# Attention with rotary embedding and a routed expert layer: probabilities turned by VectorE in 32x32 blocks, value products on eight tiles of TensorE

## The chip, the cores and the metric

One core of a Trainium2 chip. The metric is the device time of one execution in microseconds (us); the kernel before has run three times. Engines: TensorE (PE, with PEld for its weight loads), VectorE (DVE), ScalarE (ACT), GpSimd (POOL), SyncE (SP, which here only issues transfers).

## The reference

Attention over 8 batches, 8 heads, 576 positions and 64 dimensions, all float32, then a layer in which 128 tokens of each batch pass through an expert:

```python
q_rot, k_rot = rotate(q), rotate(k)            # rotary embedding
scores = np.matmul(q_rot, k_rot.transpose(0, 1, 3, 2)) / np.sqrt(D)
attn = np.exp(scores - scores.max(-1, keepdims=True))
attn = attn / (attn.sum(-1, keepdims=True) + 1e-09)
x = np.matmul(attn, v)                          # heads side by side: (B, 576, 512)
s = np.einsum('bsd,d->bs', x, w_gate)
# of each batch the 128 tokens with the highest s: x += sigmoid(s) * relu(x @ w1) @ w2
```

## The kernel before

The unit of work is a pair of heads: 32 pairs, four to a batch. For each pair, `load` (line 451) issues the transfers of k, q and v on SyncE; `rotate` (line 472) forms the rotary embedding on POOL (the first pair's on DVE); `split_qk` (line 502) splits k and q into a high and a low float32r part on ACT and on POOL or DVE. `attend` (line 528) does the attention. Its nine units (`UNITS`) are 128 queries of one head each, units 2t and 2t+1 being the two heads of query tile t, and unit 8 the last 64 queries of both heads. `units` (line 537) makes the scores of two units at a time: the two heads contract 64 dimensions on two row tiles of PE, and three products (high x high, high x low, low x high) of two halves of 288 keys go into two PSUM banks a unit. `softmax` (line 566) takes the negated maximum on DVE (`nm`), and the exponential with its sum on ACT, into `pab` (unit 8 into `pr`) in SBUF.

The value product contracts over keys, so that keys must lie on partitions, and the probabilities have queries there. `turn` (line 583) transposes a unit on PE, four blocks of 128x128 into a bank, and copies the bank to `pt` on ACT or DVE; `turn_rem` (line 607) does the last 64 keys, into `pk`. `value` (line 638) then multiplies, in two halves of the queries (c = 0 with 256 columns, c = 1 with 320): five blocks of 128 keys, for each of which the two heads run side by side on two column tiles of PE, v being the stationary operand:

```python
for kt in range(NT + 1):
    for h in range(2):
        nc.tensor.matmul(bank_of(acc)[hp, 0:n], lt, rt, start=kt == 0, stop=kt == NT)
```

Its result has dimensions on partitions; it is copied out (`ot`), transposed back on PE, and multiplied by the reciprocal sums on DVE into the output rows `x`. After each batch, `route` (line 758) ranks the tokens with many small DVE operations, gathers the 128 rows, and two chained products with `w1` and `w2` update them.

The order of all this is written by a planner (`Order`, line 71). Every operation is given engines, estimated durations, a key, and what it waits for; the planner goes through time and gives each free engine the ready operation with the lowest key, and `issue` (line 228) then emits each engine's instructions in that order, which is fixed. Keys are a time (20,000 a pair) plus offsets from the table `KEY`. `Banks` gives out the eight PSUM banks: a unit takes two neighbours ("wide"), everything else one. All instructions are recorded by one helper, so that the profile gives them one line, 211 (223 in the change).

Of the kernel before, what the change touches and what calls it, by code (L numbers as in the profile page):

```python
# [22 lines left out]
KEY = dict(ahead=6669, lag=12977, rem=76, value=4203, rows=388, load=49858, rotate=24073, half=2000,  # L23
           gate=54405, route=49769, count=21851, select=23426, turn=18811, step=10093, kstep=3, hold=2,
           patience=7975, over=350, near=3316, narrow=195)


SWITCH = ((0.0, 175.0, 194.0), (151.0, 0.0, 196.0), (151.0, 125.0, 0.0))

# [7 lines left out]

class Banks:


    def __init__(self, n):
        self.free, self.n, self.narrow = [0.0] * n, n, 0

    def when(self, kind, count=1):
        if kind == "wide":
            pairs = sorted(max(self.free[i], self.free[i + 1]) for i in range(0, self.n, 2))
            return pairs[count - 1]
        return 1e12 if self.narrow + count > KEY["narrow"] else sorted(self.free)[count - 1]

    def take(self, kind, t):  # L50
        if kind == "wide":
            i = min((max(self.free[i], self.free[i + 1]), i) for i in range(0, self.n, 2))[1]
            self.free[i] = self.free[i + 1] = 1e12
            return i
        self.narrow += 1
        i = min((self.free[i ^ 1] <= t, self.free[i], i) for i in range(self.n) if self.free[i] <= t)[2]
        self.free[i] = 1e12
        return i

    def give(self, kind, slot, at):  # L60
        self.narrow -= kind != "wide"
        for i in range(slot, slot + 1 + (kind == "wide")):
            self.free[i] = at
# [7 lines left out]
class Order:  # L71
# [26 lines left out]
    def run(self):  # L98
# [18 lines left out]
        while events:  # L117
# [4 lines left out]
            while moved:  # L122
                moved = False
                for e in names:
                    if free[e] > t:
                        continue
                    put, found, soon, first = [], None, None, None
                    while waiting[e]:
# [10 lines left out]
                        if e == "DVE" and o.mode == 2:  # L139
                            can = max(can, free["POOL"])  # L140
                        if can > t:
                            if o.urgent and can < t + KEY["patience"] and (soon is None or can < soon):
                                soon = can
                        elif soon is None or t + o.engines[e][0] <= soon + KEY["over"]:
                            if e != "PE" or o.mode == mode or (mode and o.mode):
                                found = o
                                break

                            first = first or o
                        if first and o.key > first.key + (KEY["near"] if mode else 0):  # L150
                            put.append(item)
                            break
                        put.append(item)
                    for item in put:
                        heapq.heappush(waiting[e], item)
                    found = found or first
# [5 lines left out]
                    if o is first:  # L162
                        o.done = True
# [64 lines left out]
def issue(tc, nc, order):  # L228
# [6 lines left out]
    for _, _, o, e in order:  # L235
# [5 lines left out]
        held = [i for b in o.banks for i in range(b.slot, b.slot + 1 + (b.kind == "wide"))]  # L241
        real = [i for s in held for other, i in last.get(s, {}).items() if other != e]
        keep = real + [i for a in needs.get(id(o), ()) for i in made[id(a)]]
        groups = sorted({s // 2 for s in held})
        for i in mine:
            for g in groups:
                for other in {"PE", "ACT", "DVE"} - {e}:
                    tc.declare_no_dep(i, group=f"bank{g}{other}", keep=keep, reason="other half of the tile")
# [4 lines left out]
        for i in mine:  # L253
            for g in groups:
                tc.add_to_no_dep_group(f"bank{g}{e}", i)
# [26 lines left out]
def attention_moe_kernel(ctx: ExitStack, tc: tile.TileContext, q, k, v, w_gate, w1, w2, rope, outs, cap):  # L282
# [18 lines left out]
    B, H, S, D = v.shape  # L301
    DM = H * D
    F = w1.shape[1]
    NP = H // 2
# [3 lines left out]
    KW = S + REM  # L308
    NDC = DM // P
# [14 lines left out]
    ps_banks = [ps.tile([P, 2, 512], F32, name=f"ps{i}") for i in range(4)]  # L324

    order = Order(2 * len(ps_banks))
# [33 lines left out]
    def bank_of(b):  # L360
        two = ps_banks[b.slot // 2]
        return two if b.kind == "wide" else two[:, b.slot % 2]
# [5 lines left out]
    tabk = sb("tabk", [P, 2, KW])  # L368
# [7 lines left out]
    k_ins = ring("k_in", 2, [P, 2, KW])  # L376
    rks = ring("rk", 1, [P, KW])
    rqs = ring("rq", 1, [P, KW])
    khs = ring("kh", 2, [P, KW], F32R)
    kls = ring("kl", 2, [P, KW], F32R)  # L380
    qhs = ring("qh", 2, [P, KW], F32R)
    qls = ring("ql", 2, [P, KW], F32R)
    vts = ring("vt", 3, [P, 2, NT, D])
    vrs = ring("vr", 3, [P, 2, D])
    pabs = ring("pab", 4, [P, 2 * S])
    prs = ring("pr", 1, [P, KW])
    pts = [ring(f"pt{c}", 1, [P, NT, 2, 2 * P + c * REM]) for c in range(2)]
    pks = [ring(f"pk{c}", 1, [P, 2 * P + c * REM]) for c in range(2)]
    ots = [ring(f"ot{c}", 1, [P, 2 * P + c * P]) for c in range(2)]
    xs = ring("x", 2, [P, 5, DM // 2])  # L390
    sumss = ring("sums", 3, [P, 9, 2])
    nms = ring("nm", 2, [P, 9])
    rss = ring("rs", 2, [P, 6])
# [20 lines left out]
    for t_ in vrs.tiles:  # L414
        nc.gpsimd.memset(t_[64:128, 0, :], 0.0)
        nc.gpsimd.memset(t_[0:64, 1, :], 0.0)
    nc.gpsimd.memset(ots[1].tiles[0][:, 2 * P + REM:3 * P], 0.0)
    nc.gpsimd.memset(prs.tiles[0][:, S:KW], 0.0)
# [24 lines left out]
    KCUTS, QCUTS = (0, REM + HALF, KW), (0, P, 3 * P, KW)  # L443
# [5 lines left out]
    loaded, rotated, stacks = {}, {}, {}  # L449

    def load(pi):
        b, j = divmod(pi, NP)
        key = at(pi, 0) - KEY["load"]
        main = lambda src: src[b, 2 * j:2 * j + 2, 0:512, :].rearrange("h (p t) d -> p h t d", t=NT)
        rem = lambda src, h: src[b, 2 * j + h, 512:S, :]
        kin, qin, vt, vr = k_ins.next(), q_ins.next(), vts.next(), vrs.next()
        got = {"k": [], "q": [], "v": []}
# [6 lines left out]
        for n, use, src, cuts in ("k", kin, k, KCUTS), ("q", qin, q, QCUTS):  # L464
            for i, (lo, hi) in enumerate(zip(cuts, cuts[1:]) if pi == 0 else [(0, KW)]):
                dma(n, use.tile[:, :, lo:hi], src[b, j, :, :, lo:hi], use, 2 * i + (n == "q"), 8 * P * (hi - lo))
        dma("v", vt.tile, main(v), vt, 5, 8 * P * NT * D)
        for h in range(2):
            dma("v", vr.tile[h * 64:h * 64 + 64, h, :], rem(v, h), vr, 5, 64 * 4 * D)
        loaded[pi] = (kin, qin, vt, vr, got)  # L470

    def rotate(pi):

        kin, qin, _, _, got = loaded[pi]
        first = pi == 0
        key = at(pi, 0) - KEY["rotate"]
        rk, rq = rks.next(), rqs.next()
        made = {}

        def tt(on, n, out, in0, in1, alu, after, uses, soon):  # L480
# [4 lines left out]
            for u in uses:  # L485
                u.by(o)
            return o

        for name, use, r, tab, cuts in (("k", kin, rk, tabk, KCUTS), ("q", qin, rq, tabq, QCUTS)):
            x = use.tile  # L490
            made[name] = []
            for i, (lo, hi) in enumerate(zip(cuts, cuts[1:]) if first else [(0, KW)]):
# [3 lines left out]
                       [got[name][i]] + tab_ready[name][i] if first else got[name] + sum(tab_ready[name], []), [use], soon)  # L496
                made[name].append((lo, hi, tt(
                    e, hi - lo, r.tile[:, lo:hi], x[:, 0, lo:hi], x[:, 1, lo:hi], ALU.add, [y] + r.before, [use, r], soon)))
        rotated[pi] = (rk, rq, made)


    def split_qk(pi):
        rk, rq, made = rotated.pop(pi)
# [4 lines left out]
        for n, (name, r, hu, lu) in enumerate((("k", rk, kh, kl), ("q", rq, qh, ql))):  # L508
# [564 lines left out]
```

## Time and profile before

| | |
|---|---|
| runs | 651.12 us median (649.14 to 651.22) |
| profiled execution | 648.06 us, its span 646.3 us |
| PE busy | 610.5 us, 94% |
| DVE busy | 492.8 us, 76% |
| POOL busy | 447.2 us, 69% |
| ACT busy | 413.6 us, 64% |

The span reaches from the first to the last instruction; the execution's own time is 1.7 us longer. Busy times count an engine's records, which overlap where it is pipelined. A record's duration is thus more than its share of a dense run; that share is the distance between two starts.

### The profile page before, as it was taken

How to read it: one execution, taken by the hardware profiler on the slowest of the kernel's cores; microseconds unless marked ns; L12 is line 12 of the kernel's file. 1: busy time of each engine (PE TensorE's matmuls, PEld its weight loads, DVE VectorE, ACT ScalarE, POOL GpSimd, SP SyncE). 2: the span in 40 equal slices, each digit the busy share in tenths (PEclk: the TensorE clock that was granted, in tenths of full speed). 3: DMA queues.
4: the chain of work that ended last, by engine and by line, in shares of the span. 5: the costliest groups of instructions: out<-in, count | busy, mean ns of one | idle time of the engine just before them, and what ended most of it. 6: DMA issues, size and time to landing. Idle time of an engine off the chain costs nothing.

```text
span 646.3 us, 13873 instructions
## 1 busy us (share of the span) xinstructions
PE 610.5 (94%) x5072; PEld 470.4 (73%) x5072; DVE 492.8 (76%) x1264; ACT 413.6 (64%) x989; POOL 447.2 (69%) x308
## 2 busy tenths in 40 slices
PE   3889879999999999999999999999999999999895
PEld 3567667777787777777777877877777787777574
DVE  6898878987879578885869758795878868697541
ACT  4578756777777576665776657675767657765211
POOL 4988788999998989687785678776785845300110
PEclk9999989999999999999999999999999999999999
DMA  8546514343344243333431234242332312010200
GB/s 304 183 168 217 165 57 140 125 137 120 134 142 137 75 158 99 100 119 117 144 110 56 100 127 144 83 137 71 125 124 71 119 36 72 19 38 2 70 31 18
DMA packets 38180, 71.02 MB, mean 110 GB/s; under 512 B 7776, under 2 KB 26976, under 8 KB 38112
## 3 DMA queue, kind: packets, MB, share of 16 engines
q1 hardware_dynamic: 36288, 65.29, 30.9%
q0 software_dynamic: 1280, 4.20, 1.9%
q8 instruction: 40, 0.66, 0.4%
q10 hardware_dynamic: 544, 0.66, 0.3%
q14 instruction: 28, 0.23, 0.1%
HBM read 58.59 MB, written 11.53 MB: 108 GB/s over the span
## 4 chain that ended last, share of the span: by engine, by line
PE 72%; DVE 16%; issue 6%; ACT 3%; DMA 1%; POOL 0%; POOLq 0%; DVEq 0%; ACTq 0%; SPq 0%
PE ps L211 72%; DVE nm L211 5%; DVE junk L211 4%; ACT pab L211 2%; DVE pt L211 2%; DVE x L211 1%; DVE w L211 1%; DMA k_in<-k_dram 1%; DMA xe<-w_dram 1%; DVE ql L211 0%; DVE row L211 0%; DVE ht L211 0%; DVE rs L211 0%; DVE pk L211 0%; DVE gp L211 0%
## 5 line engine op out<-in xcount | busy, mean ns | idle before, releaser
L211 DVE TENSOR_REDUCE nm<-ps 128x1 f32<-128x576 f32 x288 | 206.6, 748 | 88.1 <-PE ps L211 87.2
L211 ACT ACTIVATE pab<-ps,nm 128x576 f32<-128x576 f32 x256 | 188.1, 740 | 102.7 <-DVE nm L211 101.6
L211 PE MATMUL ps<-ident,pab 128*128 128x128 f32 x1152 | 163.0, 279 | 7.3 <-ACT pab L211 6.9
L211 PEld LDWEIGHTS ps<-ident,pab 128*128 128x128 f32 x1152 | 132.6, 143 | 20.6 <-ACT pab L211 7.5
L211 PE MATMUL ps<-pt,vt 128*64 128x320 f32 (+1 forms) x1024 | 138.2, 412 | 0.9 <-DVE pk L211 0.9
L211 ACT COPY pt<-ps 128x512 f32<-128x512 f32 x156 | 88.7, 593 | 30.9 <-PE ps L211 29.6
L211 POOL TENSOR_TENSOR k_in<-k_in,tabk 128x1280 f32<-128x1280 f32 x31 | 90.6, 2923 | 21.5 <-DMA k_in<-k_dram 21.4
L211 PEld LDWEIGHTS ps<-pt,vt 128*64 128x64 f32 x1024 | 67.9, 136 | 49.4 <-issue 8.9
L211 PE MATMUL ps<-kh,qh 64*128 64x288 f32 (+1 forms) x576 | 85.2, 344 | 13.5 <-ACT qh L211 8.1
L211 POOL TENSOR_TENSOR q_in<-q_in,tabq 128x1280 f32<-128x1280 f32 x31 | 90.9, 2933 | 5.6 <-DMA q_in<-q_dram 5.6
L211 DVE COPY pt<-ps 128x512 f32<-128x512 f32 x132 | 86.9, 680 | 6.5 <-PE ps L211 6.2
L211 PEld LDWEIGHTS ps<-kh,qh 64*128 64x128 f32 (+1 forms) x576 | 49.0, 188 | 55.5 <-ACT pab L211 22.7
L211 POOL TENSOR_TENSOR kl<-rk,kh 128x640 fp32r<-128x640 f32 x29 | 45.1, 1555 | 55.7 <-ACT kh L211 55.6
L211 PE MATMUL ps<-kh,ql 64*128 64x288 f32 (+1 forms) x576 | 69.7, 295 | 0.2 <-DVE ql L211 0.2
L211 PE MATMUL ps<-kl,qh 64*128 64x288 f32 (+1 forms) x576 | 69.2, 294 | 0.0
L211 POOL TENSOR_TENSOR prod<-x,wg 128x512 f32<-128x512 f32 (+1 forms) x45 | 49.0, 1088 | 25.8 <-DVE gp L211 18.9
L211 PE MATMUL ps<-w,xt 128*128 128x512 f32 x192 | 52.1, 412 | 1.0 <-ACT xt L211 0.7
L211 PEld LDWEIGHTS ps<-kh,ql 64*128 64x128 f32 (+1 forms) x576 | 52.4, 188 | 0.5 <-DVE ql L211 0.5
L211 PEld LDWEIGHTS ps<-kl,qh 64*128 64x128 f32 (+1 forms) x576 | 52.4, 188 | 0.0
L211 PE MATMUL ps<-w,ht 128*128 128x512 f32 x192 | 51.3, 406 | 0.5 <-DVE ht L211 0.5
L211 POOL TENSOR_TENSOR rq<-q_in 128x640 f32<-128x640 f32 x31 | 48.5, 1565 | 3.7 <-DVE ql L211 3.5
L211 ACT ACTIVATION_READ_ACCUMULATOR pab<-ps,nm 128x1 f32 x256 | 50.9, 199 | 0.0
(98 smaller groups left out, 809.9 us busy)
## 6 DMA issues: line engine op xcount, KB each, us to landing
k_in<-k_dram SPq DMA_DIRECT2D x31, 640.0 KB, 3.8
q_in<-q_dram SPq DMA_DIRECT2D x31, 640.0 KB, 4.3
vt<-v_dram SPq DMA_DIRECT2D x32, 256.0 KB, 2.7
out_dram<-x SPq DMA_DIRECT2D x16, 512.0 KB, 3.4
xe<-w_dram SPq DMA_DIRECT2D x8, 256.0 KB, 3.5
row<-w_dram SPq DMA_DIRECT2D x8, 256.0 KB, 3.1
vr<-v_dram SPq DMA_DIRECT2D x64, 16.0 KB, 2.4
out_dram<-x SPq DMA_DIRECT2D x16, 64.0 KB, 3.1
```

Of the source, the lines that this page charges most:

```text
L211: i = made(*args, **kwargs)
```

## The change

Probabilities no longer pass through PE to be turned. The nine units of a pair lie in one tile `prob` of 128 partitions by nine slots of 576, two such tiles in turn. Behind each exponential DVE transposes the slot in place, in blocks of 32x32: within each group of 32 partitions a block then has keys on partitions and queries along it. `turn` and `turn_rem`, `pab`, `pr`, `pt` and `pk` are gone.

`value` runs once a pair. The block of 32 keys number kb lies in all four partition groups a, there for the 32 queries a of each query tile. Each group is a row tile of PE (32 rows), and each head a column tile (64 columns), so that there are eight products for each of 18 key blocks, of five or four slots of 32 columns (160 or 128), and each row tile adds up in a PSUM bank of its own: four neighbouring banks, 0 to 3, a new kind "quad". v is needed on all four partition groups, so the host lays it out four times (`_by_key`), and it is loaded in two halves (`load_v`).

```diff
+            y = op({"DVE": dve(S)}, lambda: nc.vector.transpose(dst, dst), key + KEY["lag"], [x])
+            prob.by(x, y)
+            turned.append(y)
+
+        def value(key, late):
+            acc, b, br = Bank("quad"), Bank("t"), Bank("t")
...
+            def products(i):
+                for c in range(NB // 2):
+                    for a in range(4):
+                        for h in range(2):
+                            hp, ap = slice(64 * h, 64 * h + 64), slice(32 * a, 32 * a + 32)
+                            s0, s1 = (0, NT + (a < 2)) if h == 0 else (NT + (a < 2), U)
+                            to = 32 if s0 != NT else 0
+                            kb = i * NB // 2 + c
+                            nc.tensor.matmul(
+                                bank_of(acc)[hp, a, to:to + 32 * (s1 - s0)].rearrange("p (s c) -> p s c", c=32),
+                                vt[i].tile[ap, c, h, :], prob.tile[ap, s0:s1, kb * 32:kb * 32 + 32],
+                                start=kb == 0, stop=kb == NB - 1)
+
+            o = None
+            for i in range(2):
+                o = op(pe(NB // 2 * 280), lambda i=i: products(i), key, turned + [got[i], o], acc, mode=1)
...
-                dma("v", vt.tile, main(v), vt, 5, 8 * P * NT * D)
...
+            o = op(LOAD, lambda use=use, src=src: nc.sync.dma_start(use.tile, src),
+                   at(pi, 0) - KEY["load"] + 5 + i, use.before, moved=8 * P * NB // 2 * D)
...
+def _by_key(v):
+    B, H, S, D = v.shape
+    t = v[:, :, _columns(S)].reshape(B, H // 2, 2, S // 32, 32, D).transpose(0, 1, 4, 3, 2, 5)
+    return np.tile(t, (1, 1, 4, 1, 1, 1))
```

Smaller edits: k loses 64 doubled columns (640 to 576), the rotated k and q overwrite their input tiles instead of `rk` and `rq`, output rows are scaled in one operation for four query tiles and one for the rest, `KEY` has other values, and the planner may leave PE in its tiling mode at a cost taken from that table (`STAY`). While a quad waits for its banks, other work gets banks 4 to 7 only.

What the planner makes of it, on DVE in the second pair of heads. `nm` are maxima, `pt` and `pk` copies of transposed probabilities, `rs` reciprocal sums. Before:

```order
L211 TENSOR_REDUCE nm_115<-ps_64 128x1
L211 COPY pt_103<-ps_66 128x4x128
L211 COPY pk_105<-ps_63 128x256
L211 COPY pt_104<-ps_63 128x8x64
L211 TENSOR_REDUCE nm_115<-ps_65 128x1
```

and now, `prob` being the probabilities:

```order
L223 TENSOR_REDUCE nm_99<-banks 128x1 x4
L223 STREAM_TRANSPOSE prob_91<-prob_91 128x576
L223 TENSOR_REDUCE nm_99<-banks 128x1 x2
L223 STREAM_TRANSPOSE prob_91<-prob_91 128x576 x2
L223 TENSOR_REDUCE rs_101<-sums_96 128x9
```

The copies between the maxima have given way to block transposes; over the whole program 288 of them come, and 132 copies into `pt` on DVE and 156 on ACT go.

On PE, at the end of a pair, `ident` being the identity against which a block is transposed. Before, the first pair:

```order
L211 MATMUL ps_65<-ident,pr_102 128x128 x4
L211 MATMUL ps_65<-ident,pab_101 128x128 x8
L211 MATMUL ps_64<-ident,pab_100 128x128
L211 MATMUL ps_64<-ident,pab_101 128x128
L211 MATMUL ps_64<-ident,pr_102 128x128 x2
L211 MATMUL ps_64<-pt_104,vt_92 64x320 x8
L211 MATMUL ps_64<-pk_106,vr_95 64x320 x2
L211 MATMUL ps_66<-kh_85,qh_89 128x288
```

and now, a later pair, the scores of the next one and then the first key block:

```order
L223 MATMUL banks<-kh_80,qh_84 128x288 x4
L223 MATMUL banks<-kl_82,qh_84 128x288 x4
L223 MATMUL banks<-kh_80,ql_86 128x288 x4
L223 MATMUL banks<-prob_90,vt_88 64x160
L223 MATMUL banks<-prob_90,vt_88 64x128
L223 MATMUL banks<-prob_90,vt_88 64x160
L223 MATMUL banks<-prob_90,vt_88 64x128 x2
L223 MATMUL banks<-prob_90,vt_88 64x160
L223 MATMUL banks<-prob_90,vt_88 64x128
L223 MATMUL banks<-prob_90,vt_88 64x160 x2
```

The transposes that stood ahead of the value products are gone, and the products, ten of 256 and ten of 320 columns a pair, are now 144 of 128 or 160.

The end of the last batch on DVE. `junk` are comparisons that rank tokens of the batch before the last, `x` output rows, `ht` a hidden layer's low part. Now, behind the last maximum:

```order
L223 TENSOR_REDUCE nm_99<-banks 128x1 x2
L223 TENSOR_TENSOR x_94<-banks,rs_100 128x4x128
L223 TENSOR_TENSOR x_94<-banks,rs_100 64x128
L223 STREAM_TRANSPOSE prob_91<-prob_91 128x576
L223 SCALAR_TENSOR_TENSOR junk_121,gp_104<-x_94,wg 128x128
...
L223 TENSOR_REDUCE rs_101<-sums_96 64x1
L223 RECIPROCAL rs_101<-rs_101 128x10
L223 STREAM_TRANSPOSE prob_91<-prob_91 128x576
L223 TENSOR_SCALAR junk_122,cnt_111<-row_110,sc_109 128x320
L223 TENSOR_SCALAR junk_122,cnt_111<-row_110,sc_109 128x384
```

Before, those comparisons stood some forty rows ahead of the last maximum; now five of them, the rank and the selection come behind it, as do the last two transposes.

## Rows read from the trace of the kernel before

**Rows 1.** The page's head, busy times and the SyncE queue
```profile
span 646.3 us, 13873 instructions
...
PE 610.5 (94%) x5072; PEld 470.4 (73%) x5072; DVE 492.8 (76%) x1264; ACT 413.6 (64%) x989; POOL 447.2 (69%) x308
...
q1 hardware_dynamic: 36288, 65.29, 30.9%
```

**Rows 2.** The page's chain that ended last, by engine
```profile
PE 72%; DVE 16%; issue 6%; ACT 3%; DMA 1%; POOL 0%; POOLq 0%; DVEq 0%; ACTq 0%; SPq 0%
```

**Rows 3.** Groups by shape: operands, shapes, count | busy us, mean ns | idle before, releasers
```profile
L211 DVE TENSOR_REDUCE nm<-ps 128x1 f32<-128x576 f32 x288 | 206.6, 748 | 88.1 <-PE ps L211 87.2 <-ACT pr L211 0.6
...
L211 PE MATMUL ps<-ident,pab 128*128 128x128 f32 x1152 | 163.0, 279 | 7.3 <-ACT pab L211 6.9 <-DVE x L211 0.2
...
L211 DVE COPY pt<-ps 128x512 f32<-128x512 f32 x132 | 86.9, 680 | 6.5 <-PE ps L211 6.2
...
L211 DVE TENSOR_TENSOR x<-ps,rs 128x256 f32<-128x256 f32 x64 | 26.5, 415 | 4.6 <-PE ps L211 4.6
...
L211 DVE TENSOR_REDUCE gp<-prod 128x2 f32<-128x512 f32 x30 | 20.1, 669 | 0.0
...
L211 DVE TENSOR_TENSOR ht<-ps,ht 128x512 fp32r<-128x512 f32 x16 | 10.9, 683 | 8.1 <-ACT ht L211 8.0
...
L211 DVE TENSOR_TENSOR ql<-rq,qh 128x640 fp32r<-128x640 f32 x6 | 7.2, 1206 | 0.0
```

**Rows 4.** PE's timeline, merged: start us, us, engine, operation, count [idle before]
```profile
87.42 0.66 PE L211 MATMUL ps<-ident,pab 128*128 128x128 f32 x4 [3.49 <-ACT pab L211]
...
305.36 0.27 PE L211 MATMUL ps<-tok,sel 128*128 128x5 bf16 x5
305.49 0.42 PE L211 MATMUL ps<-ident,pab 128*128 128x128 f32 x2
...
307.66 2.38 PE L211 MATMUL ps<-pt,vt 128*64 128x320 f32 x16
...
310.50 0.53 PE L211 MATMUL ps<-kh,qh 64*128 64x288 f32 x4
...
312.32 2.01 PE L211 MATMUL ps<-ident,pab 128*128 128x128 f32 x16
314.17 0.60 PE L211 MATMUL ps<-ident,pr 128*128 128x128 f32 x4
...
316.12 1.95 PE L211 MATMUL ps<-pt,vt 128*64 128x256 f32 x16
...
318.43 0.53 PE L211 MATMUL ps<-kh,qh 64*128 64x288 f32 x4
```

**Rows 5.** PE's timeline of 307.66 to 307.67 us
```profile
307.66 0.49 PE L211 MATMUL ps<-pt,vt 128*64 128x320 f32 x2
```

**Rows 6.** DVE's timeline, early and late
```profile
46.33 2.73 DVE L211 TENSOR_REDUCE nm<-ps 128x1 f32<-128x576 f32 x4
...
58.32 2.47 DVE L211 COPY pt<-ps 128x512 f32<-128x512 f32 x4
...
595.25 0.74 DVE L211 TENSOR_REDUCE nm<-ps 128x1 f32<-128x576 f32 x1
...
608.78 0.17 DVE L211 TENSOR_REDUCE sc<-gp 128x5 f32<-128x15 f32 x1
```

**Rows 7.** Windows: busy us (instructions) of PE, PEld, DVE, ACT, POOL, clock, DMA
```profile
0.00:11.80 11.80, 2.59 (x18) 2.24 (x20) 7.03 (x31) 4.35 (x9) 2.67 (x20) 1.00 0.83 288
11.80:596.00 584.20, 568.06 (x4852) 438.52 (x4850) 465.65 (x1151) 399.43 (x960) 438.12 (x278) 1.00 0.34 112
596.00:646.30 50.30, 39.80 (x210) 29.64 (x208) 20.14 (x85) 9.82 (x20) 6.39 (x11) 0.96 0.12 39
40.00:60.00 20.00, 18.11 (x168) 14.29 (x169) 18.79 (x35) 15.93 (x40) 18.77 (x12) 1.00 0.47 151
80.00:100.00 20.00, 16.40 (x135) 12.48 (x133) 15.97 (x25) 11.11 (x30) 18.07 (x10) 0.91 0.27 92
```

More of the change, by code (lines that the diff above doesn't have):

```diff
@@ L144, in run @@
                         elif soon is None or t + o.engines[e][0] <= soon + KEY["over"]:
[L145 to L151, printed above, removed]
+                            late = o.key + (STAY[mode][o.mode] if e == "PE" else 0)
+                            if first is None or late < least:
+                                first, least = o, late
+                        put.append(item)
+                        if first and o.key >= least:
                             break
-                        put.append(item)
+                    found = first
                     for item in put:
-                        heapq.heappush(waiting[e], item)
-                    found = found or first
+                        if item[2] is not found:
+                            heapq.heappush(waiting[e], item)
                     if found is None:
@@ L240, in issue @@
             continue
-        held = [i for b in o.banks for i in range(b.slot, b.slot + 1 + (b.kind == "wide"))]
+        held = [i for b in o.banks for i in range(b.slot, b.slot + WIDTH[b.kind])]
         real = [i for s in held for other, i in last.get(s, {}).items() if other != e]
         keep = real + [i for a in needs.get(id(o), ()) for i in made[id(a)]]
-        groups = sorted({s // 2 for s in held})
         for i in mine:
-            for g in groups:
-                for other in {"PE", "ACT", "DVE"} - {e}:
-                    tc.declare_no_dep(i, group=f"bank{g}{other}", keep=keep, reason="other half of the tile")
+            for other in {"PE", "ACT", "DVE"} - {e}:
+                tc.declare_no_dep(i, group=f"banks{other}", keep=keep, reason="other banks of the tile")
         for r in {r.name for r in real}:
@@ L253, in issue @@
         for i in mine:
[L254 to L255 removed]
+            tc.add_to_no_dep_group(f"banks{e}", i)
         for s in held:
@@ L322, in ring @@
         return Ring([sb(f"{name}{i}", shape, dtype) for i in range(n)])
-    ps_banks = [ps.tile([P, 2, 512], F32, name=f"ps{i}") for i in range(4)]
-    order = Order(2 * len(ps_banks))
+    banks = ps.tile([P, 8, 512], F32, name="banks")
+    order = Order(8)
     op = order.op
@@ L638, in value @@
-        def value(c, key, late):
-            n = 2 * P + c * REM
-            acc, b = Bank("t"), Bank("t")
-            ot, rs = ots[c].next(), rss.next()
-            def products():
-                for kt in range(NT + 1):
-                    for h in range(2):
-                        hp = slice(64 * h, 64 * h + 64)
-                        lt, rt = ((vt.tile[:, h, kt, :], pt[c].tile[:, kt, h, :]) if kt < NT
-                                  else (vr.tile[:, h, :], pk[c].tile))
-                        nc.tensor.matmul(bank_of(acc)[hp, 0:n], lt, rt, start=kt == 0, stop=kt == NT)
-            o = op(pe((NT + 1) * 2 * (n * 2 / 2.4 + 2.5)), products, key, evacs[c] + got["v"], acc, mode=1)
-            for use in (vt, vr, pt[c], pk[c]):
-                use.by(o)
-            e = op(either(n), lambda e: copy(e, ot.tile[:, 0:n], bank_of(acc)[:, 0:n]), key, [o] + ot.before, acc)
-            w = 4 + c
+            y = op({"DVE": dve(S)}, lambda: nc.vector.transpose(dst, dst), key + KEY["lag"], [x])
@@ L666, in value @@
             sums.by(rr)
             def turns():
-                for i in range(2 + c):
-                    nc.tensor.transpose(bank_of(b)[:, i * P:i * P + P], ot.tile[:, i * P:i * P + P], ident)
-            if j % 2 == 0 and c == 0:
+                for t in range(NT):
+                    nc.tensor.transpose(bank_of(b)[:, t * P:t * P + P], ot.tile[:, t * P:t * P + P], ident)
+                nc.tensor.transpose(bank_of(br)[0:REM, 0:P], ot.tile[:, 512:S], ident)
+            if j % 2 == 0:
```

283 lines of the change are left out of this document (119 added, 164 removed).

## The prediction

> **What bounds the kernel now.** I read the page's busy times first: TensorE (PE) is busy 610.5 us of 646.3, VectorE (DVE) 492.8 [rows 1]. The chain that ended last agrees: 72% of it is PE, 16% DVE [rows 2]. So until now a microsecond taken off PE counts, and one added to DVE does not. The question is how far that holds once the change takes from PE and gives to DVE; for that I need both engines' sums after the change, and the stretches at both ends in which neither is full. The groups by shape [rows 3] give the prices on DVE, the timelines [rows 4 to 6] the pace of operations that follow one another closely, and the windows [rows 7] the ends. Durations of single instructions overlap, so I price a run by its pace wherever a timeline shows one.
>
> **PE.** Per pair of heads 42 transposes of probabilities go (36 from pab, 6 from pr). Sixteen take from 312.32 to 314.17, so 116 ns each [rows 4]; 42 x 32 x 0.116 = 155 us go. The old value products took 318.43 - 316.12 = 2.31 us for the half of 256 columns and 310.50 - 307.66 = 2.84 us for that of 320 [rows 4], 5.15 us a pair. The new ones are 18 key blocks of eight products each, on eight tiles. No row shows eight tiles. The nearest is the 320-column run: ten products on two column tiles in 2.84 us, so one tile needs 0.568 us for 320 columns and 0.284 for 160. If all eight run side by side, a key block costs 0.284 us, a pair 5.11; if four do, 0.568 and 10.2; if only two, as today, 1.136 and 20.4. I take the lower end: a float32 product makes two records, one for each pass (16 for the first eight products [rows 4]), and yet the two column tiles of today start within 0.01 us of each other [rows 5], so a tile doesn't wait for its neighbour's second pass; and row tiles already run two abreast in the scores. Then PE has 610.5 - 155.4 = 455 us of work, products unchanged. The five output transposes of a pair stay five.
>
> By contrast a floor on starts would hurt: the five 5-column products of sel start from 305.36 to 305.49, 26 ns apart, however small they are [rows 4]. Sixteen passes a key block (two for each float32 product) at 26 ns are 0.416 us, 7.5 us a pair, and PE has 455 + 32 x 2.4 = 532 us. The Trainium skill states this floor ("TensorE: Matmul & The Clock Gate", section "Wait — 56ns, not 53.3ns?"): starts never come closer than about 25 ns, whatever the columns. The 0.01 us between two tiles [rows 5] speaks against its holding across tiles, but there no long stream was tested, so it remains a rival.
>
> **DVE.** Removed by the counts in the order: 132 copies into pt, 86.9 us [rows 3]. The row multiplications go from 64 of 128x256 (26.5 us) to 32 of 128x512, priced by the ht row of the same shape and source, 32 x 0.683 = 21.9: 4.6 less [rows 3]. Edits under 13 us each (the pk copies, half of the reciprocals and sums' reductions, ot copies that go to ScalarE, low parts and routing copies that change engine), taken the same way from the counts and their rows' means, make 47.7 together. So 492.8 - 139.2 = 353.6 us stay.
>
> Added are 288 block transposes of 128x576 float32, 9 a pair. No row shows one. Nearest is the maximum nm, also one input of 576 per partition: four in 2.73 us, the last lasting 0.75, so 0.66 apart; and the copies of 512, four in 2.47, 0.60 apart [rows 6]. A one-input operation that reads SBUF instead of PSUM, gp<-prod, takes 669 ns for 512 against 680 for the copy [rows 3]: SBUF costs nothing extra. I take 0.67, 193 us, and DVE has 547. The lower bound is 0.60 (173 us). The upper is the row of an operation in SBUF that reads two inputs beside GpSimd (POOL): ql, 1.206 us for 640 [rows 3], 347 us.
>
> The Trainium skill has a rule here ("SBUF — State Buffer", section "SBUF: two separate sides"): a DVE operation with two SBUF inputs or in a two-port mode excludes POOL's for its whole duration. The slow ql row fits it; gp<-prod, one input, shows no such stretch.
>
> **Which ends last.** DVE 547 against PE 455: the bound passes to DVE, whose sum I now lay over the span. First maximum at 11.80 us, last one ending at 596.0, end at 646.3 [rows 6, 7]. Of DVE's work 7.0 us lie ahead of the first maximum and 20.1 behind the last [rows 7]. In the change about 9 us more come behind it (order of the last batch: two transposes, seven routing counts and selections of batch 6 that formerly stood ahead). Between the maxima remain 547 - 7 - 29 = 511. DVE's densest stretch now, 40 to 60 us, is busy 18.79 of 20, 94% [rows 7]. 511 / 0.94 = 543.
>
> The start costs 11.8 as now. At the end the value products of the last pair come in one piece after its last transpose: maximum, exponential, the DVE work that stands ahead of that transpose in the order (5 us), products 5.1, evacuation, transposes, rows and gates (5) make 15.5 us up to the row of sc, where 608.78 - 596.0 = 12.8 was spent [rows 6]; so 53 for 50.3. Sum: 11.8 + 543 + 53 = 608. The profiled execution took 1.7 us over its span, so 610; the median of the runs shown is 651.12 where that execution had 648.06, 0.5% more: **612**.
>
> **What lies beside this.** v is replicated over four partition groups and loaded as 1.18 MB a pair instead of 0.29; with k 64 columns narrower, the DMA total goes from 65 MB to about 92 on SyncE's queue, whose packets now fill 30.9% of the engines [rows 1]; at 44% it hides behind a pair's 17 us. At the start DMA is busy 0.83 of the time [rows 7] and the first v is 0.9 MB longer, but first used only after the first pair's nine units. POOL loses a tenth of the k work and gains four ql of 1.6 us. ScalarE (ACT) loses 156 pt copies and stays below DVE. Where DVE is late, the maxima are late, and PE, in-order, waits at the next scores: this cannot cost more than DVE's share already charges.
>
> **Rivals.**
> - *Floor on starts*: PE at 532 of a 610-us run, nearly as full as DVE. Of the 2.4 us a pair that its products grow, between none and all (77 us) shows; I take a third, 25 us: 637. For it the 26 ns; against it the two tiles that start together. The granted clock could do the same: PE stood idle 3.49 us before 87.42 [rows 4], and the granted clock of 80 to 100 us is 0.91, a stretch at the lower of its two levels (1.2 GHz for 2.4) [rows 7]. A PE that waits for DVE more often may lose it more often; the lower level for a tenth of its work is 46 us of PE time, again mostly inside the 92 that lie between it and DVE.
> - *Four tiles abreast*: PE 455 + 32 x 5.1 = 618, more than DVE, and with today's 36 us unfilled [rows 1] 654 in all, 656 to 660 as a median: no gain or slightly slower. The point where it decides is about 0.55 us a key block.
> - *Two abreast*: 455 + 32 x 15.3 = 945, plus 36: 981.
> - *Transposes that collide with POOL*, the slower one: each waits for, or is slowed by, a POOL operation as the two-input ql is. POOL is busy 69% [rows 1], so most would meet one. At 1.206 us DVE has 701, between the maxima 665 / 0.94 = 707, with the ends 772. It decides from (646.3 - 11.8 - 53) x 0.94 = 547 = 318 + 288 t, that is t = 0.80 us. For it: ql. Against it: gp<-prod, and that a transpose has one input.
>
> **How the numbers follow.** DVE bound with eight tiles abreast: 62%, its own range 592 (transposes at 0.60, DVE 94% busy between the maxima) to 637 (0.67 and 90%). Starts or clock: 14%, 612 to 650. Four abreast: 7%. Collision: 8%. Two abreast: 4%. Better than 590: 5%. The range takes in the first three, 590 to 662, 83%, leaving 12% above and 5% below. A change of under 0.3% (2 us) can't be told from none in this kernel's runs. Faster by more: 62 + 5 and 12 of the 14: 79%. Same: 2 of the 14 and 2 of the 7: 4%. Slower: 17%.
>
> **What would show it.** In the new profile DVE should be busiest, near 547 us, PE near 455 to 470 with some 11,700 matmul records, ACT near 320. 288 block transposes of DVE with a mean record near 0.74 us and a pace of 0.66 confirm the price; 1 us and more refute it. Key blocks 0.28 us apart confirm the tiles; 0.42 is the floor, 0.57 four abreast. The chain should be mainly DVE; if PE holds over half of it, I was wrong on the bound. The forecast fails as a whole if DVE's share between first and last maximum is below 88%, for then waits, not work, set the time.

## The result, and the profile after

The changed kernel takes 657.54 us (median of 10 runs, 652.54 to 662.31) where the kernel before took 649.39: ratio 1.0121, 95% interval 1.0085 to 1.0157. The forecast was 612 us with a chance of 0.79 for faster; the time lies inside its range of 590 to 662, the sign is wrong. The profiled execution took 657.86 us.

The page of the kernel after, lines that answer to [rows 1] and [rows 2]:

```profile
span 656.1 us, 26406 instructions
...
PE 522.9 (80%) x11664; PEld 436.4 (67%) x11664; DVE 560.7 (85%) x1241; ACT 329.5 (50%) x814; POOL 436.6 (67%) x306
...
PEclk9988587787898997999989997899989996999799
...
q8 instruction: 91, 1.49, 0.9%
...
PE 50%; DVE 22%; ACT 10%; issue 9%; DMA 4%; POOL 3%; POOLq 0%; SPq 0%; DVEq 0%; ACTq 0%
```

DVE came out near the forecast (560.7 us for 547), PE did not: 522.9 for 455. No engine is full, and the chain still has PE on half of it. The row of the granted clock, nearly flat before, now has slices down to 5; by the trace's record of the clock, TensorE ran at its lower level (1.2 GHz) in 17 stretches, 111 us of the span, against 3 stretches and 8 us before. Groups of the same page, as in [rows 3] (busy us, mean ns, then the idle time ahead of them and what ended it):

```profile
L223 DVE TENSOR_REDUCE nm<-banks 128x1 f32<-128x576 f32 x288 | 203.7, 744 | 47.4 <-PE banks L223 46.4
L223 PE MATMUL banks<-prob,vt 32*64 32x160 f32 (+1 forms) x9216 | 211.6, 322 | 39.5 <-issue 16.0
...
L223 DVE STREAM_TRANSPOSE prob<-prob 128x576 f32<-128x576 f32 x288 | 204.9, 746 | 0.6 <-ACT prob L223 0.5
L223 PE MATMUL banks<-kh,qh 64*128 64x288 f32 (+1 forms) x576 | 91.0, 363 | 70.1 <-ACT prob L223 42.9
```

The block transposes cost what was priced: 746 ns a record, 0.71 us each in busy time. But DVE waits 46 us for scores (nm <- PE), PE waits 43 us for exponentials ahead of scores, and 16 us stand ahead of value products with no releaser ("issue"), 6.1 of them in a single wait at 25 us.

Windows of the kernel after, to be laid beside [rows 7] (busy us and instructions of PE, PEld, DVE, ACT, POOL; clock; DMA share; GB/s):

```profile
11.82:596.00 584.18, 474.62 (x11190) 398.76 (x11189) 527.54 (x1100) 315.56 (x784) 428.75 (x284) 0.92 0.49 159
596.00:656.10 60.10, 45.69 (x461) 35.46 (x461) 26.18 (x112) 9.62 (x21) 6.39 (x11) 0.90 0.10 33
350.00:400.00 50.00, 45.11 (x1083) 37.32 (x1083) 48.81 (x112) 29.03 (x71) 40.38 (x28) 1.00 0.48 150
100.00:150.00 50.00, 35.88 (x755) 30.50 (x755) 43.27 (x90) 25.97 (x66) 40.44 (x27) 0.80 0.45 148
```

The last two maxima on DVE:

```profile
596.00 1.42 DVE L223 TENSOR_REDUCE nm<-banks 128x1 f32<-128x576 f32 x2 [1.41 <-PE banks L223]
```

The first two windows part where these begin; the last maximum ends at 597.43 us, where it ended at 595.99 before. So the middle, up to that end, took 585.6 us for 584.2, and 8.4 of the 9.8 us lie in the end, 58.7 for 50.3. Against the forecast (11.8 + 543 + 53) the middle is 43 too long and the end 6. In the middle the kernel loses early and wins late: the first ten pairs end 15 us later than before (the next maximum is at 198.3 us, for 183.4), while three full batches further on (first maxima of the 17th to the 29th pair) take 215.4 us for 225.8.

Two things are seen in PE's own timeline of the kernel after. First the gaps:

```profile
301.55 0.49 PE L223 MATMUL banks<-prob,vt 32*64 32x128 f32 x4 [0.97 <-issue]
301.96 0.53 PE L223 MATMUL banks<-kh,qh 64*128 64x288 f32 x4
302.34 0.42 PE L223 MATMUL banks<-kl,qh 64*128 64x288 f32 x4
302.60 0.43 PE L223 MATMUL banks<-kh,ql 64*128 64x288 f32 x4
302.96 2.18 PE L223 MATMUL banks<-prob,vt 32*64 32x160 f32 x112
305.55 0.80 PE L223 MATMUL banks<-prob,vt 32*64 32x160 f32 x32 [0.41 <-issue]
```

Between the two gaps lie 4 + 12 + 112 = 128 records. The page counts 11,664 products and as many weight loads in 91 fetches of instructions (q8, 1.49 MB): 256 instructions a fetch, or 128 records. The fetch ahead of the first gap stands alone in the DMA view of 298.4 to 300.2 us: it begins at 298.65 and takes 5.0% of 16 engines' 1.8 us, 1.45 us, and 1.45 us behind its end the gap ends. It is the same over the whole trace. Counting products, weight loads and the few entries of PE's sequencer in order, 15 of the 21 waits without a releaser, 13.9 us, stand at place 192 or 193 of every 256, whatever operation comes next, and each ends 1.2 to 1.5 us behind the end of a fetch; the six others are the one of 6.1 us at 25 us and five short ones, 1.3 us in all. So PE stops where a block of instructions ends and the next has not come. The Trainium skill gives blocks of this size ("Advanced Engine Details and Errata", section "ISA Cache": a cache line of 16 KB, which is 256 instructions). The trace agrees: 1.49 MB in 91 fetches are 16 KB each. Then the clock:

```profile
132.26 4.35 PE L223 MATMUL banks<-prob,vt 32*64 32x160 f32 x144 [0.36 <-ACT prob L223]
...
137.53 2.73 PE L223 MATMUL banks<-prob,vt 32*64 32x160 f32 x144
```

The first half of the pair's products runs mostly at 1.2 GHz (until 135.62), the second at 2.4. Ahead of the fall at 121.97 PE had been busy 3.2 of the 5.0 us from 117 on, waiting for DVE and exponentials; ahead of one at 43.46, 3.2 of the 7.5 us from 36 on. The Trainium skill ("TensorE: Matmul & The Clock Gate", section "A second HAM failure mode: psum-queue depth-cycling") describes such behaviour in another kernel, which cycles through PSUM banks: short pauses between groups of products, and a clock that goes back and forth. The trace agrees, with its 17 stretches.

From the starts of the value products' records I take their price apart. Their 61 unbroken runs last 203.6 us from first to last start. At full clock 16 records take 0.272 us, which makes 155.6; 1690 records ran at the lower level at 0.533 per 16, which adds 27.6 (136 of them, at 25 to 29.8 us, are known by this pace alone: the trace's record of the clock begins behind them); 20.4 remain. Of these, stalls of 0.2 us and more between two starts make 16, 12 of them at the ends of blocks. Up to the next instruction's start, or the last product's end where PE then waits, the runs hold PE for 217.9 us.

### The profile page after: what moved, and what is told of

It is laid out like the page before. It is cut to its first block, busy times and chain, and to the rows that moved or that the text cites. A ratio compares the mean times of both kernels' runs of the same rounds, so it can differ in the third digit from the quotient of the medians.

```text
span 656.1 us, 26406 instructions
## 1 busy us (share of the span) xinstructions
PE 522.9 (80%) x11664; PEld 436.4 (67%) x11664; DVE 560.7 (85%) x1241; ACT 329.5 (50%) x814; POOL 436.6 (67%) x306
## 3 DMA queue, kind: packets, MB, share of 16 engines
q0 software_dynamic: 1280, 4.20, 1.8%
q8 instruction: 91, 1.49, 0.9%
## 4 chain that ended last, share of the span: by engine, by line
PE 50%; DVE 22%; ACT 10%; issue 9%; DMA 4%; POOL 3%; POOLq 0%; SPq 0%; DVEq 0%; ACTq 0%
PE banks L223 50%; DVE nm L223 8%; ACT prob L223 7%; DVE prob L223 5%; DVE x L223 3%; DMA row<-w_dram 3%; ACT ot L223 2%; DMA q_in<-q_dram 2%; DVE junk L223 2%; POOL q_in L223 1%; POOL k_in L223 1%; DVE rs L223 1%; POOL w L223 1%; ACT qh L223 1%; DVE xe L223 1%
## 5 line engine op out<-in xcount | busy, mean ns | idle before, releaser
L223 ACT ACTIVATE prob<-banks,nm 128x576 f32<-128x576 f32 x288 | 211.3, 739 | 195.0 <-DVE nm L223 194.2
L223 DVE TENSOR_REDUCE nm<-banks 128x1 f32<-128x576 f32 x288 | 203.7, 744 | 47.4 <-PE banks L223 46.4
L223 PE MATMUL banks<-prob,vt 32*64 32x160 f32 (+1 forms) x9216 | 211.6, 322 | 39.5 <-issue 16.0
L223 PEld LDWEIGHTS banks<-prob,vt 32*64 32x64 f32 x9216 | 185.9, 145 | 59.1 <-issue 31.1
L223 DVE STREAM_TRANSPOSE prob<-prob 128x576 f32<-128x576 f32 x288 | 204.9, 746 | 0.6 <-ACT prob L223 0.5
L223 PE MATMUL banks<-kh,qh 64*128 64x288 f32 (+1 forms) x576 | 91.0, 363 | 70.1 <-ACT prob L223 42.9
L223 POOL TENSOR_TENSOR k_in<-k_in,tabk 128x1152 f32<-128x1152 f32 x31 | 82.3, 2654 | 0.0
L223 PE MATMUL banks<-kh,ql 64*128 64x288 f32 (+1 forms) x576 | 75.9, 317 | 0.6 <-POOL ql L223 0.3
L223 PE MATMUL banks<-kl,qh 64*128 64x288 f32 (+1 forms) x576 | 75.1, 314 | 0.7 <-issue 0.7
L223 PEld LDWEIGHTS banks<-kh,ql 64*128 64x128 f32 (+1 forms) x576 | 57.9, 207 | 1.4 <-POOL ql L223 1.0
L223 ACT COPY ot<-banks 64x64 f32<-64x64 f32 (+1 forms) x93 | 27.7, 333 | 34.7 <-PE banks L223 33.8
```

The lines of the kernel that those rows point to most:

```text
L223: i = made(*args, **kwargs)
```

## The experiments

Theories, as the expectations name them: W, DVE's work sets the time; C, the clock; S, the supply of instructions; B, too few PSUM banks for scores while the four accumulators are held. Unless said otherwise a run is the changed kernel with one edit. The kernel before ran beside each, with medians of 648 to 650 us.

### Value products with half the instructions

```diff
-                for c in range(NB // 2):
+                for c in range(i, NB // 2, 2):
...
-                            s0, s1 = (0, NT + (a < 2)) if h == 0 else (NT + (a < 2), U)
+                            s0, s1 = 0, U
```

> Value products of every second key block are left out, and those that stay take all nine query tiles (288 columns instead of 160 or 128), so TensorE streams the same number of columns with half the value instructions (4608 records instead of 9216); the output is another one. Theory S (gaps without a releaser inside runs of value products, 20.7 us between 20 and 600 us, are instructions that come late): the gaps go, VectorE idles 12 to 20 us less, 638 to 646 us. Theories C, B and W: 652 to 662.

Measured: 618.15 us (616.06 to 618.44), ratio to before 0.9509 (0.9479 to 0.9539). Far more than expected, but the edit was not clean: 9 runs of 288 columns are shorter than 18 of 160, on the tiles that end last. So the same with equal streaming:

```diff
-                for c in range(NB // 2):
+                for c in range(i, NB // 2, 2):
...
-                                vt[i].tile[ap, c, h, :], prob.tile[ap, s0:s1, kb * 32:kb * 32 + 32],
+                                vt[i].tile[ap, c, h, :], prob.tile[ap, s0:s1, kb * 32:kb * 32 + 64],
```

> Value products of every second key block are left out, and each that stays takes 64 columns of a query tile instead of 32 (320 or 256 columns instead of 160 or 128; another output): half the value instructions, and this time exactly the same streaming time on the slowest tile (9 x 320 for 18 x 160 columns), which the run with 288 columns did not have (9 x 288 is a tenth less, 17 us in all by its 0.485 us per 16 records against 2 x 0.272). Theory S (instructions that come late): the gaps without a releaser, 20.7 us, go, and the time falls to 632 to 642 us. If the 39 us of that run came from its shorter streaming: 648 to 658.

Measured: 621.93 us (617.59 to 624.71), ratio 0.9584 (0.9528 to 0.964). Its page:

```profile
PE 496.9 (80%) x7056; PEld 382.2 (62%) x7056; DVE 556.9 (90%) x1241; ACT 329.0 (53%) x814; POOL 436.2 (70%) x306
...
q8 instruction: 55, 0.90, 0.6%
...
DVE 41%; PE 32%; ACT 9%; issue 7%; DMA 4%; POOL 4%; POOLq 0%; ACTq 0%; DVEq 0%
```

PE's waits in the same kernel and, below, in the kernel after, both from 20 to 600 us (waited for: us, times, longest):

```profile
PE banks L223 <- issue: 6.3, 1, 6.3
```

```profile
PE banks L223 <- issue: 20.7, 19, 6.1
```

One long wait of 6 us is in both and is no gap of this kind; the other 18, 14.6 us, are gone. Five runs below and above have half the value instructions, and none has a wait at the end of a block; the ten others have 9 to 23 each. The value runs hold PE, up to the next instruction's start, for 188.9 us instead of 217.9, 29 less, and the kernel is 35.6 us faster (657.54 - 621.93): value product time counts in full. S is shown, and larger than its gaps: by an estimate with the sums above, some 18 of the 29 us are stalls and 7 the lower level, at which 613 records of double length ran for 1690 (granted clock 0.933 for 0.915). The edit halves the weight loads as well; that it is the supply that stalls is told by the place of the gaps. Now DVE leads the chain, as forecast for the change itself, and the time is within 10 us of that forecast. That the run before, with 16 us less value time (172.7), gains only 4 us more fits a bound that has passed on.

### Four tiles instead of eight

```diff
-                    for a in range(4):
+                    for a in (0, 2):
```

> Row tiles 1 and 3 of the value products are left out (another output), the order and the four banks stay: the same number of value instructions and the same streaming time per tile as in the run with 64 columns of each tile, but four tiles of the array side by side instead of eight. Theory C (the clock falls with what TensorE does, and a low clock costs time): a granted clock below 0.85, and 35 us or more over that run. If the clock does not matter to the time: within 6 us of that run, whatever the granted clock.

Measured: 710.7 us (710.49 to 715.73), ratio 1.0983 (1.0934 to 1.1032), 89 us above the run with 64 columns, at a granted clock of 0.765. Page, and DVE's first wait:

```profile
PE 604.1 (85%) x7056; PEld 510.8 (72%) x7056; DVE 557.9 (79%) x1241; ACT 330.0 (47%) x814; POOL 436.1 (62%) x306
...
PEclk9566656556775699559986799558997897669699
```

```profile
DVE nm L223 <- PE banks L223: 94.9, 41, 5.5
```

As many value instructions, the same streaming time on each tile, the same order; only half the tiles, and no gaps. The value runs hold PE for 249.5 us for 188.9, because 2381 of 4608 records ran at 1.2 GHz (613 there), and the score products lengthen too (busy times of their three groups 270.0 us for 235.0). C is shown as a mechanism: what PE loses to the lower level is paid on the path. What share of the changed kernel's own time it is, this pair of runs does not show.

### Accumulators in two banks

```diff
-WIDTH = {"t": 1, "wide": 2, "quad": 4}
+WIDTH = {"t": 1, "wide": 2, "quad": 2}
...
-                    for a in range(4):
+                    for a in range(2):
```

> Row tiles 2 and 3 of the value products are left out (half of the keys), so the accumulators take two banks instead of four, and while they are held three pairs of banks are left for scores instead of two; VectorE's work is the same, TensorE has half the value instructions as in the run with half the instructions, in the same time per key block if the tiles run side by side. Theory B (only one pair of units fits beside the accumulators, so VectorE waits for the next maxima while products run): VectorE's idle time between first and last maximum falls from 56.7 to under 30 us, 620 to 632 us, and clearly below the run with half the instructions. Theory S: the same as that run. Theories C and W: 648 to 660.

Measured: 711.59 to 733.61 us in four runs, clock 0.767 in the profile, which is of the longest. The edit halves the tiles as the last one does, and so lowers the clock as much; beside that run (710.7 us), the right one to compare, even the shortest gains nothing from a third pair of banks, and DVE waits for scores ahead of maxima as long (93.4 us for 94.9). Since the planner also made a new order, B is not supported rather than refuted.

### Without the block transposes

```diff
-            y = op({"DVE": dve(S)}, lambda: nc.vector.transpose(dst, dst), key + KEY["lag"], [x])
+            y = op({"DVE": dve(S)}, lambda: None, key + KEY["lag"], [x])
```

> The 288 block transposes are left out (the products read the probabilities unturned; another output); everything else stays in its order. VectorE has 560.7 - 204.9 = 356 us. Theory W (the added VectorE work sets the time): TensorE's 523 us becomes the longest, of which some 40 us are the low clock, so 530 to 585 us. Theories B, C, S together (waits around the products set the time, VectorE's work only fills them): 600 us or more.

Measured: 639.43 us (two runs), ratio 0.9847 (0.9796 to 0.9898):

```profile
PE 509.5 (80%) x11664; PEld 425.1 (67%) x11664; DVE 375.0 (59%) x953; ACT 329.3 (52%) x814; POOL 436.9 (69%) x306
...
PE 57%; ACT 11%; DVE 10%; issue 10%; POOL 7%; DMA 3%; POOLq 0%; DVEq 0%; ACTq 0%
```

DVE lost a third of its busy time (375.0 us for 560.7) and the kernel 18 us. W falls. With half the instructions as well:

> Both at once: the 288 block transposes are left out and the value products have half the instructions at the same streaming time (64 columns of each tile). If two limits lie one behind the other (the value instructions' supply first, 36 us; VectorE's added work behind it, hidden until the first is gone): the gain of leaving out the transposes, 18 us alone, grows to 35 us or more on top of the other, 570 to 587 us. If TensorE's waits for banks and exponentials set the time in any case: 600 to 620.

Measured: 597.67 us (594.85 to 598.19), ratio 0.9194 (0.9165 to 0.9223). The transposes are worth 24 us here (621.93 - 597.67), not the 35 of two limits one behind the other, and 2 us under the other theory's band. PE holds 52% of that chain and ACT 16%, at 82% and 55% busy. What is left looks like PE and the exponentials waiting for each other; no run tests it.

### The gate sums on ScalarE

```diff
-                   lambda t0=t0, t1=t1, n=n, prod=prod: nc.vector.tensor_reduce(
-                       gp.tile[0:n, t0:t1, i], prod.tile[0:n, 0:t1 - t0], axis=AX.X, op=ALU.add),
+                   lambda t0=t0, t1=t1, n=n, prod=prod: [nc.scalar.activation(
+                       prod.tile[0:n, t - t0], prod.tile[0:n, t - t0], AF.Copy,
+                       accum_out=gp.tile[0:n, t, i:i + 1]) for t in range(t0, t1)],
```

Once planned anew as ScalarE work, once at the old place in every order:

> The 45 sums of the gate products (gp from prod, 25.3 us of VectorE) go to ScalarE, which is busy half of the time; all results stay. Theory W (VectorE's work sets the time): 25 us less on VectorE, 630 to 640 us. If TensorE and its waits set the time, as the run without the transposes suggests (205 us of VectorE taken away, 22 us gained): 650 to 660.

> As the run with the gate sums on ScalarE, but every other instruction keeps its place in the order of all engines (the planner still counts them as VectorE's): 25.3 us of VectorE's 560.7 go, all results stay. If VectorE's work sets the time: 630 to 640. If the value products on TensorE do (supply and clock): 648 to 658. Over 670 would say that ScalarE's order, not VectorE's sum, decides.

Measured: 703.96 us (699.94 to 710.93) planned anew, 653.74 (650.72 to 657.44; ratio 1.0085, 1.0054 to 1.0117) at the old place. 25 us of DVE's work are worth 4 us, which is hardly clear of the scatter (the two ratios' intervals overlap). The first of the two tells of the order alone: there ACT waits 116.8 us for value products ahead of `ot` copies (33.8 in the kernel after).

### Against the gaps and the low clock

Four pieces instead of two, products cut where the instruction blocks end, idle places filled, and a fourth score term in the first ten pairs:

```diff
-            for i in range(2):
+            for i in range(len(CUTS) - 1):
```

> The value products of a pair are given to the planner in four pieces of 5, 4, 5 and 4 key blocks instead of two of 9; all results stay. Theory B (scores wait behind 2.5 to 5 us of products, and VectorE behind the scores): VectorE's idle time between the maxima falls from 56.7 to under 35 us, 630 to 645 us; theory S agrees in part (shorter runs of short instructions), some 640 to 650. If neither, 652 to 662.

Measured: 676.28 us (671.75 to 678.42). Of the waits without a releaser the long one at 25 us is gone, but at the ends of blocks there are 14.3 us, as many as in the changed kernel (13.9), and PE waits longer for exponentials (PE <- ACT prob 82.7 for 62.8): neither theory.

```diff
-                for c in range(NB // 2):
+                for kb in range(0, CUT[pi]) if i == 0 else range(CUT[pi], NB):
```

> As the run before, and each pair's value products are cut after 6 to 13 of the 18 key blocks instead of always after 9, chosen so that the scores between the two pieces come within the 95 products ahead of every 256th instruction of TensorE, where the gaps without a releaser stand; all results stay. Theory S: gaps fall from 21 us to 10 to 14, and the time by 5 to 12 us against that run, 640 to 650, level with or below the kernel before the change. If the gaps do not come from the supply of instructions: no change against that run.

Measured: 660.93 us (657.11 to 661.63), 7 above the run with the sums at their place. At the ends of blocks PE waits 21.3 us for 15.7 there, and 13 of the 23 waits now stand ahead of scores or other products (5 of 16 there). The idea behind the cuts does not hold: scores put where a block ends wait for the next block as value products do.

```diff
+                fill("S", bank_of(b_)[:, 0, 384:512], FILL_S.get(seen["S"], 0))
                 for i, n, first, last, lt, rt in mms:
```

> In 50 places where the changed kernel's TensorE waited over 0.4 us (ahead of scores for the second pair of banks, ahead of value products for the last transpose), 740 bfloat16 products of 128 columns are issued into columns that nobody reads of a bank that TensorE already owns: some 40 us of work laid into its 110 us of waiting between first and last maximum; nothing else is moved. Theory C (clock: an idler TensorE falls to 1.2 GHz in 17 stretches, 113 us, and its slow products make VectorE wait): the granted clock rises from 0.915 to 0.96 or more and the time falls to 632 to 646 us. Theories B (banks), S (instruction supply) and W (VectorE's own work): the clock may rise, the time stays at 651 to 662.

Measured: 684.11 us (682.04 to 687.08), ratio 1.0525 (1.0482 to 1.0568), clock 0.922. The fillers waited themselves (PE before <- ACT prob 52.1 us) and were then paid for: 57 us of PE work in places of waiting cost 27. It tells nothing of the clock, and once more that PE time is on the path.

```diff
-            for a, b in ((qh, kh), (qh, kl), (ql, kh)):
+            for a, b in ((qh, kh), (qh, kl), (ql, kh)) + (((ql, kl),) if pi < 10 else ()):
```

> As the run with the gate sums at their place, and in the first ten pairs, where TensorE has no expert work and the granted clock is lowest (pairs 1 to 9 of that run: 20 to 202 us, mean some 0.8), each score product gets the fourth term (ql by kl), a quarter to a third more score work in the place where TensorE waits for banks anyway; results stay within rounding. Theory C for this stage: the clock of the stretch rises above 0.9, and the ten pairs, 190.7 us in that run, take 5 to 15 us less: 638 to 649. If the clock there only follows the waiting and costs nothing: the added products, 10 x 5 x 0.25 us, are hidden or cost up to 8 us: 652 to 662.

Measured: 655.21 us (652.96 to 657.69), against 653.74. In the one profile of each, the clock of 11.8 to 200 us rose from 0.78 to 0.88 and the first ten pairs ended 5 us earlier (197.2 for 202.4); but in that of the changed kernel itself they end at 198.3 at a clock of 0.85, and the whole took no less. That a better clock pays in this stage is not shown.

### Other prices in the planner

```diff
-                o = op(pe(NB // 2 * 280), lambda i=i: products(i), key, turned + [got[i], o], acc, mode=1)
+                o = op(pe(NB // 2 * 340), lambda i=i: products(i), key, turned + [got[i], o], acc, mode=1)
...
-KEY = dict(ahead=3680, lag=35838, value=1507, ...
+KEY = dict(ahead=-2313, lag=40704, value=487, ...
```

> The run with the gate sums on ScalarE, planned anew with prices from the profile: a key block of value products 0.340 us instead of 0.280 (203.6 us first to last start, over 32 x 18 key blocks, is 0.353), block transposes 0.712, maxima 0.690; the table KEY is searched for these prices (offsets, no other edit). All results stay. If part of the loss is that the order counts on value products that the chip does not deliver, and so leaves VectorE and TensorE waiting for each other: 620 to 643 us, below the kernel before. If the waits come from the bank and exponential chain or the clock, whatever the order: 648 to 665; 670 and more as the other two runs that were planned anew (704, 676) if orders found on paper miss the chip in any case.

> The same prices, another table found for them, with other offsets for loads, routing and experts: same expectations as the run before (620 to 643, or 648 to 665, or 670 and more); both together show whether it is the prices or the luck of one table.

> The same prices and a third table found for them: the same expectations, 620 to 643 us if the prices of the order matter, 648 to 665 or more if not.

Measured: 669.93 (669.77 to 674.33), 674.98 (671.57 to 675.86) and 670.87 us (668.42 to 677.08). All three are 16 to 21 us above the order they started from, that of the run with the sums at their place: in effect the third of the three outcomes. In the first, value runs hold PE no shorter (215.0 us for 211.6 there) and PE waits longer for exponentials (79.0 for 61.3). Of all runs that keep the results, none beats the kernel before.

## Why the prediction was wrong

**What held.** Transposes at 0.67 to 0.71 us each and no collision with POOL; eight tiles abreast, 0.272 us a key block for 0.284; the start, 11.8 us; DVE's sum to 14 us; ACT below DVE; DMA hidden.

**The step that failed** is the one on the bound: "DVE 547 against PE 455: the bound passes to DVE", and with it the sentence that PE's waiting "cannot cost more than DVE's share already charges". Taking the transposes (205 us of records, 186 of busy time) off DVE gains 18, taking 29 off PE's value runs gains 36. PE's 92 us under DVE were no cover. The waits suggest why: scores, maxima, exponentials and products of neighbouring pairs hand the same eight banks on in a fixed order, so that DVE runs out of scores while PE is in its products (46 us), and PE waits for exponentials to leave the banks while DVE catches up (43 us). No run shows this by itself, and a third pair of banks did not help.

**Luck.** The time lies inside 590 to 662, but not by the forecast's reasons: its likeliest case ended at 637, and the top of the range was kept for four tiles abreast (656 to 660), while eight ran abreast.

**The term that was mis-sized** is the value products. Priced at 5.11 us a pair, up to the next instruction's start, 163.5 us; so counted, the runs hold PE for 217.9: 155.6 at full clock, 27.6 for the lower level, 20.4 for stalls, 14.3 behind the last starts. The three groups of score products, which the forecast left alone, are busy 184.8 us together for 170.1 before, also by the clock: 205 of their 1728 records ran at the lower level, for 12 before. The span is 48 us over the forecast's 608; on paper the 54 and the 15 us cover it, with DVE's work between the maxima, 18 us above its 511, lying mostly beside them. The run that halves the instructions fits this: value runs 188.9, time 622, inside the band of the forecast's likeliest case, 592 to 637. The gaps were in no rival. What spoke for them stood in the change: 9216 value records for 1280; half a pair was ten products in 2.84 us [rows 4] and is 72 in 2.7.

**The clock rival** had its mechanism right ("a PE that waits for DVE more often may lose it more often") and its weight wrong. Its 46 us were to be covered by PE's slack, so that a third would show; 14% was too little.

**DVE's share** between the maxima was to be 94%, taken from the densest stretch of before; it is 529.0 / 585.6 = 90%, above the 88% named as the point of failure. That test was badly chosen: DVE was 90% busy and not the bound, as the run without transposes shows; its static order lets it work while PE's lateness decides when the work comes free. The better sign was the other one named, PE on over half of the chain: it stood at the edge, 50%.

**The end** was to grow by 2.7 us and grew by 8.4. PE's timeline, behind the last transpose, which ends at 601.67 us:

```profile
600.59 2.59 PE L223 MATMUL banks<-w,ht 128*128 128x512 f32 x10 [0.26 <-DVE ht L223]
604.79 1.15 PE L223 MATMUL banks<-prob,vt 32*64 32x160 f32 x46 [1.60 <-DVE xe L223]
606.27 3.55 PE L223 MATMUL banks<-prob,vt 32*64 32x160 f32 x98 [0.34 <-issue]
```

The products waited for the expert layer of the batch before, which held one of the four banks until DVE had added its rows (`xe`), 3.1 us that the forecast did not have; then they took 9.0 us instead of 5.1, with gaps and, from 606.66 to 610.07 us, at the lower level.

What stays open: how much of the 27.6 us of low clock could be had back in this kernel by itself. Four tiles against eight show that the clock counts on this path; the two attempts to hold it up cost as much as they could bring. That late fetches cause the gaps rests on the gaps' place in every block of 256, on the fetch that ends shortly before each gap does, and on the runs with half the instructions; why a fetch comes in time at one block and late at another is not shown. How the banks tie DVE and PE together is read from waits, not tested.

## What to carry to other kernels

Price a stream of many small products by its instructions too: count records per fetch and look for waits without a releaser at that distance. Slack of an engine is cover only if the other engine has work queued that does not depend on it; between engines that hand banks to one another in a fixed order, charge the slower time of the one that feeds at full price, and take the clock that its new pauses will bring into that price. And before a re-planned experiment is read, run the same edit with the old order.

## What the runs showed of the hardware

- In the kernel after, 15 gaps of 0.15 to 2.5 us, 13.9 us in all, each at the same place in a block of 256 of PE's instructions and each ending 1.2 to 1.5 us behind the end of an instruction fetch, in three pairs of heads exactly 128 records apart; a dense run of 32-row products takes 128 records in 2.2 us. At half the value instructions there is none.
- A lower granted clock with a busier PE: 0.765 at 85% busy in the run with four tiles, 0.933 at 80% with eight. In the first of these, at 205.49 us, it fell inside an unbroken run of 72 value records, behind a wait of 1.85 us; the next such run, at the lower level, took 5.08 us (2.67 at the full one).
- Times scattered more where the clock wandered: 1.5% over ten runs of the kernel after, 0.4% over ten of the one before.
